# Two sets of seven products for a blocked second layer: which operands are summed first, and on which engine

## The chip, the cores and the metric

The kernel runs on one core of one Trainium2 chip. The metric is the device time of one execution in microseconds (us); the figure for a kernel is the median of its runs. The engines are named as in the profile: PE is TensorE (matmuls), PEld its weight loads, DVE is VectorE, ACT is ScalarE, POOL is GpSimd, SP is SyncE, which only issues transfers here.

## The reference, cut to what matters

```python
# q, k, v: 8 batches x 8 heads x 576 positions x 64
scores = scale * q @ k^T                      # per batch and head
ret    = (scores * Dmat) @ v                  # Dmat[i, j] = gamma_h ** (i - j) for i >= j, else 0
x      = ret, heads side by side              # 4608 tokens x 512
h      = x @ w_in                             # 512 -> 2048
g      = h * cos(h)
out    = g @ w_out                            # 2048 -> 512, float32
```

## The kernel before, in words

The 4608 tokens are worked off in ten stages, n = 0 to 9, of 512 tokens each but for n=1 and n=2, which have 256. A stage first runs the first layer (`mm1`, L365) in eight blocks. A block is 1024 columns of PSUM (two banks); in a late stage it holds two groups of 128 features by 512 tokens, eight matmuls in all. ScalarE takes the cosine (L373, as a sine with a shifted argument), VectorE multiplies (L374) and writes bf16 into the tile `gT`. Only then is the PSUM bank free. The blocks go round three bank pairs, `abmabmab`, so block i+3 waits for the multiplication of block i. The tile `gT` holds all 16 feature groups `et`. From n=4 on the order of the blocks alternates between the lower half of the features (`et` 0 to 7) and the upper half (8 to 15): blocks 0, 2, 4, 6 are the lower half, 1, 3, 5, 7 the upper.

From n=3 (`S7`) on the second layer is not computed as one product but by seven half-sized ones in the manner of Strassen. g is cut into quarters by token half (256 tokens each) and feature half, w_out into quarters by feature half and column half (256 columns each). Sums of quarters of w_out are made once (`w_sums`, L418), sums of quarters of g in each stage (`g_sum`, L445, tiles `gs..`). A product (`product`, L517) is 16 matmuls of 128x256 into one PSUM bank, `n` or `st`. In the kernel before the order is 3, 4, 5, 2, 1, 7, 6. Products 3 and 4 read `gT` itself; products 5, 2, 1, 7 and 6 each read a sum, so there are five sums a stage. Sum 5 is on VectorE, in two instructions of 1024 elements, one after block 3 and one late; nearly all of the other four go to GpSimd in instructions of 512 elements. The first GpSimd sum after a VectorE sum is made to wait for it (the `gate`). Where the results go, ScalarE copies three of them out of PSUM per stage (L557, L564, L569) and VectorE does six additions (L537, L559); the results leave in four stores (L544).

`sums_after(n, i)` places the sums behind block i. `late_sums(n)` places the second halves. `mm2_seven` issues the products; its `at` table hangs the attention work of later token groups between the products: `unit7` makes two state products (L266, VectorE sums `s` at L287), the attention output (L319, L333) and two groups of scores (L195), which VectorE masks (L207) into `ret`. With n=5 to 8 there are two such units; in n=3 and 4 a further group of scores comes first, and the last unit uses bank `b`. The list `pend` holds VectorE work that is issued at the next `flush`.

`store` issues a store on SP and calls `feed`, which for n>=3 prepares further token groups: three GpSimd instructions per group, scaling q (L140), scaling k (L140) and casting v (L156; on ScalarE for the last ten groups), one transposing DMA per group (L167) and loads of later groups (L117). SP issues in order, so a store that waits holds up the transposes and loads behind it. Each of `gT` and the `gs` tiles exists once. The schedule is the program's order on each engine.

Of the kernel before, what the change touches and what calls it, by code (L numbers as in the profile page):

```python
# [8 lines left out]
F32 = mybir.dt.float32  # L9
# [4 lines left out]
ALU = mybir.AluOpType  # L14
# [3 lines left out]
def kernel(  # L18
# [112 lines left out]
    def prep(g, early=False, kv_first=False):  # L131
# [20 lines left out]
        if early:  # L152
            tiles["fv", g] = fv
        else:
            copy_v = nc.scalar.copy if g > starts[S7] // P + 17 else nc.gpsimd.tensor_copy
            copy_v(vb, fv)  # L156
            if c == MIX and g > PER:
                copy_v(v_odd[HP:, g // PER % 2], fv[HP:])
# [245 lines left out]
    def w_sums(x, e0, e1):  # L404

        a, b, op_ = {
            3: ((0, 1), (1, 1), ALU.subtract),
            4: ((1, 0), (0, 0), ALU.subtract),
            1: ((0, 0), (1, 1), ALU.add),
            6: ((0, 0), (0, 1), ALU.add),  # L410
            7: ((1, 0), (1, 1), ALU.add),
        }[x]
        if x in (3, 4):
            w_sum[x] = w_quarter(*a)
        elif x not in w_sum:
            pool, tag = {1: (consts, "ws1"), 6: (first, "qs4"), 7: (first, "qT4")}[x]
            w_sum[x] = pool.tile([P, E2, N2], BF16, tag=tag, name=f"ws{x}")
        nc.vector.tensor_tensor(  # L418
            out=w_sum[x][:, e0:e1],
            in0=w_quarter(*a)[:, e0:e1],  # L420
            in1=w_quarter(*b)[:, e0:e1],
            op=op_,
        )

    def g_sum(n, x, e0, e1):

        gT = tiles["g", n]
        a, b, op_ = {
            5: ((0, 0), (0, 1), ALU.add),
            2: ((1, 0), (1, 1), ALU.add),  # L430
            1: ((0, 0), (1, 1), ALU.add),
            7: ((0, 1), (1, 1), ALU.subtract),
            6: ((1, 0), (0, 0), ALU.subtract),
        }[x]
        if ("gs", n, x) not in tiles:
            tiles["gs", n, x] = sump.tile([P, E2, 256], BF16, tag=f"gs{x}", name=f"gs{x}")
        on_dve = x == 5 or (n, x) == (S7, 2) or (n, x, e0) in (
            (S7, 1, 4), (last, 1, 0), (last, 2, 4)
        )
        step = e1 - e0 if on_dve else 2  # L440
        for e in range(e0, e1, step):
            i0, i1 = (
                gT[:, k * E2 + e : k * E2 + e + step, r * 256 : (r + 1) * 256] for r, k in (a, b)
            )
            i = (nc.vector if on_dve else nc.gpsimd).tensor_tensor(  # L445
                out=tiles["gs", n, x][:, e : e + step], in0=i0, in1=i1, op=op_
            )
            if on_dve:
                tiles["gate"] = i
            elif "gate" in tiles:  # L450
                tc.add_manual_dep(
                    i.ins,
                    tiles.pop("gate").ins.name,
                    mybir.DependencyInfo(mybir.DependencyClass.Sync, mybir.DependencyReason.DATA),
                    reason="port free",
                )

    def sums_after(n, i):

        if n == S7:  # L460
            if i < 4:
                w_sums(3 + i % 2, i // 2 * 4, i // 2 * 4 + 4)
            elif i < 6:
                g_sum(n, 5, i % 4 * 4, i % 4 * 4 + 4)
                if i == 5:
                    g_sum(n, 6, 0, 4)
            elif i == 7:
                g_sum(n, 2, 0, E2)
                g_sum(n, 1, 4, E2)
                g_sum(n, 1, 0, 4)  # L470
                for e in (0, 4):
                    g_sum(n, 7, e, e + 4)
                prep_next(kv_first=True)
                g_sum(n, 6, 4, E2)
        elif n == S7 + 1 and i in (3, 7):
            for x in (5, 2, 1):
                g_sum(n, x, i - 3, i + 1)
            for x in (7, 6) if i == 7 else ():
                for e in (0, 4):
                    g_sum(n, x, e, e + 4)  # L480
        elif i == 3:
            for x in (5, 2, 1, 7, 6) if n < last else (5, 1, 2, 7, 6):
                g_sum(n, x, 0, 4)
        elif i == 7 and n == last:
            late_sums(n)

    def late_sums(n):
        for x in (5, 2, 1, 7, 6):
            g_sum(n, x, 4, E2)

    def product(n, x):
# [3 lines left out]
        if x in (3, 4, 7) or (x == 1 and n < last):  # L495
            ps = psum.tile([P, 2, N2], F32, tag={3: "n", 4: "st", 1: "n", 7: "st"}[x], name="o")
            tiles["o", x] = [ps[:, j] for j in range(2)]
            tiles["all", x] = ps
        elif x == 1:
            ps = psum.tile([P, N2], F32, tag="n", name="o")  # L500
            pt = psum.tile([P, 2, 512], F32, tag="a", name="o")
            tiles["o", x] = [ps] + [pt[:, k, : N2 // 2] for k in range(2)]
        if x in (1, 6) and n == last:
            parts = [(0, 0, N2), (1, 0, N2 // 2), (1, N2 // 2, N2)]
        dst = tiles["o", {5: 3, 2: 4, 6: 1}.get(x, x)]
        lhs = {3: gT[:, :E2, :256], 4: gT[:, E2:, 256:]}.get(x)
        if lhs is None:
            lhs = tiles["gs", n, x]
        rhs = {5: w_quarter(1, 1), 2: w_quarter(0, 0)}.get(x)
# [5 lines left out]
        for e, i in order:  # L515
# [5 lines left out]
                start=(x in (3, 4, 1, 7) and e == 0 and (i == 0 or len(parts) > 2)),  # L521
# [5 lines left out]
    def mm2_seven(n, at):  # L527
# [8 lines left out]
        def add(out_, in0, in1, op_=ALU.add):  # L536
            pend.append(lambda: nc.vector.tensor_tensor(out=out_, in0=in0, in1=in1, op=op_))  # L537

        def new(tag):
            return op.tile([P, 2, N2], F32, tag=tag, name="ot")  # L540

        def store(t, r, c, s):
            r0 = starts[n] + r * 256
            nc.sync.dma_start(  # L544
                out[r0 : r0 + 256, c * N2 : (c + 1) * N2].rearrange("(j p) c -> p j c", p=P), t
            )
            feed(s)

        for x in (3, 4, 5, 2, 1, 7, 6):
            if x in at:  # L550
                at[x](flush, pend)
            else:
                flush()
            parts = product(n, x)
            if x == 3:
                u22 = new("a")
                nc.scalar.copy(u22, tiles["all", 3])  # L557
            elif x == 4:
                pend.insert(0, lambda: nc.vector.tensor_tensor(  # L559
                    out=u22, in0=tiles["all", 4], in1=u22, op=ALU.add  # L560
                ))
            elif x == 5:
                c12, u11 = new("c"), new("b")
                nc.scalar.copy(c12, tiles["all", 3])  # L564
                add(u11, u22, tiles["all", 3], ALU.subtract)
                store(c12, 0, 1, s0)
            elif x == 2:
                c21 = new("d")
                nc.scalar.copy(c21, tiles["all", 4])  # L569
                add(u22, u22, tiles["all", 4], ALU.subtract)  # L570
                store(c21, 1, 0, s0 + 1)
            elif x == 1 and n < last:
# [311 lines left out]
```

## Time and profile before

| what | value |
| --- | --- |
| time, median of three runs | 299.81 us (298.25 to 300.58) |
| span of the profiled execution, first to last instruction | 298.2 us |
| mean granted TensorE clock | 1.000 |
| busy: PE, DVE, ACT, POOL | 287.1, 207.9, 135.9, 209.4 us |
| sums of g on POOL (L445, 102 instructions) | 116.3 us, 1180 ns each |
| sums of g on DVE (L445, 18 instructions) | 20.4 us |
| multiplications into `gT` on DVE (L374, 72 instructions) | 87.8 us, 1223 ns each |
| final additions on DVE (L537 128x512 in two groups, and L559) | 13.1 + 9.6 + 4.8 us |

For the profiled execution only its span is given; it ran as long as the fastest of the three timed runs. A time of an engine is the union of its instructions; the matmuls' ends are modelled. In timeline lines the first number is the start in us from the begin of the span, the second the length in us, "x" the number of merged instructions, and the bracket tells how long the engine was idle before and what ended it. A line of the waits gives who waited for whom, the total in us, how often, and the longest.

### The profile page before, as it was taken

Reading aid. Unit: us, or ns where it says so; the run is one execution under the profiler, and the core shown is the slowest. Engines: PE = TensorE matmul, PEld = TensorE weight load, DVE = VectorE, ACT = ScalarE, POOL = GpSimd, SP = SyncE. Lnnn points to the kernel's source line nnn. Section 1 sums busy time; section 2 is a strip of 40 time slices with the busy share of each in tenths; the row PEclk is TensorE's granted clock in tenths of the full one; section 3 lists DMA queues with packets and bytes.
Section 4 is the critical chain, followed back from the end, with each engine's and each line's share of the span. In section 5 each row is a group of like instructions: output and inputs, shape, how many; then the busy total and the mean of one; then the engine's idle time right before and its main releaser. Section 6 shows DMA issues by size and latency. Waiting matters only on the chain.

```text
span 298.2 us, 7384 instructions
## 1 busy us (share of the span) xinstructions
PE 287.1 (96%) x3113; PEld 195.3 (65%) x3113; DVE 207.9 (70%) x245; ACT 135.9 (46%) x167; POOL 209.4 (70%) x214
## 2 busy tenths in 40 slices
PE   8899999999999999979999999999999999999995
PEld 3478646848578786448744875488448845874584
DVE  5677637564579994788848874887489757935872
ACT  2656433514255432642346554546464446425620
POOL 2750066436445599997999999599959946980693
PEclk9999999999999999999999999999999999999999
DMA  7999999999999999999999997998690260031013
GB/s 203 212 209 206 209 214 213 200 243 208 208 174 222 211 239 213 217 279 176 198 224 229 209 200 183 212 208 201 122 194 2 73 143 0 2 106 36 0 44 99
DMA packets 154304, 50.28 MB, mean 169 GB/s; under 512 B 140832, under 2 KB 153248, under 8 KB 154272
## 3 DMA queue, kind: packets, MB, share of 16 engines
q1 hardware_dynamic: 149504, 45.10, 77.2%
q0 software_dynamic: 4224, 4.19, 8.5%
q8 instruction: 24, 0.39, 0.6%
q10 hardware_dynamic: 544, 0.52, 0.5%
q14 instruction: 8, 0.07, 0.1%
HBM read 36.70 MB, written 9.44 MB: 155 GB/s over the span
## 4 chain that ended last, share of the span: by engine, by line
PE 43%; POOL 25%; SPq 13%; DMA 8%; DVE 5%; issue 3%; ACT 1%; POOLq 0%; DVEq 0%
PE h L365 22%; POOL gs L445 17%; PE o L517 11%; SPq L117 8%; POOL qks L140 6%; PE o L382 5%; SPq L167 4%; DVE gT L374 3%; DMA fk<-in_k_dram 2%; DMA w_in_sb<-in_moe_w_in_dram 2%; DMA qkT<-qks 2%; POOL vb L156 2%; DVE gs L445 2%; DMA fv<-in_v_dram 1%; ACT cosh L373 1%
## 5 line engine op out<-in xcount | busy, mean ns | idle before, releaser
L445 POOL TENSOR_TENSOR gs<-gT 128x512 bf16<-128x512 bf16 x102 | 116.3, 1180 | 29.4 <-DVE gs L445 29.4
L365 PE MATMUL h<-xT,w_in_sb 128*128 128x512 bf16 (+2 forms) x832 | 127.6, 313 | 2.6 <-DVE gT L374 1.8
L374 DVE TENSOR_TENSOR gT<-h,cosh 128x1024 bf16<-128x1024 f32 x72 | 87.8, 1223 | 43.7 <-ACT cosh L373 40.7
L373 ACT ACTIVATE cosh<-h,half_pi 128x1024 f32<-128x1024 f32 x72 | 80.2, 1114 | 72.2 <-PE h L365 69.8
L365 PEld LDWEIGHTS <-w_in_sb 128*128 128x128 bf16 x832 | 75.9, 98 | 51.6 <-issue 3.0
L140 POOL TENSOR_TENSOR qks<-fq,gq 128x512 bf16<-128x512 f32 x32 | 34.0, 1062 | 40.9 <-DMA fq<-in_q_dram 40.9
L517 PEld LDWEIGHTS <-gs 128*128 128x128 bf16 x576 | 53.6, 98 | 10.1 <-POOL gs L445 2.9
L140 POOL TENSOR_TENSOR qks<-fk,gk 128x512 bf16<-128x512 f32 x35 | 37.3, 1066 | 8.0 <-DMA fk<-in_k_dram 7.4
L207 DVE TENSOR_TENSOR ret<-sc,tri 128x1024 bf16<-128x1024 f32 x32 | 38.1, 1217 | 2.8 <-PE sc L195 2.7
L517 PE MATMUL o<-ws,gs 128*128 128x256 bf16 (+1 forms) x352 | 39.1, 268 | 0.7 <-POOL gs L445 0.5
L382 PE MATMUL o<-w_out_sb,gT 128*128 128x512 bf16 x128 | 30.1, 380 | 0.0
L517 PE MATMUL o<-w_out_sb,gT 128*128 128x256 bf16 x224 | 26.6, 273 | 0.1
L517 PE MATMUL o<-w_out_sb,gs 128*128 128x256 bf16 x224 | 26.1, 273 | 0.5 <-POOL gs L445 0.4
L537 DVE TENSOR_TENSOR ot<-o,ot 128x512 f32<-128x512 f32 (+2 forms) x25 | 14.9, 603 | 14.7 <-PE o L517 14.5
L517 PEld LDWEIGHTS <-gT 128*128 128x128 bf16 x224 | 21.4, 98 | 4.7 <-DVE gT L374 0.7
L350 ACT CAST xT<-ov 128x1024 bf16<-128x1024 f32 (+1 forms) x18 | 16.5, 917 | 16.1 <-PE ov L319 13.9
L445 DVE TENSOR_TENSOR gs<-gT 128x1024 bf16<-128x1024 bf16 (+1 forms) x18 | 20.4, 1148 | 0.3
L382 PEld LDWEIGHTS <-gT 128*128 128x128 bf16 x128 | 11.8, 98 | 12.5
L156 POOL CAST vb<-fv 128x512 bf16<-128x512 f32 x22 | 14.3, 651 | 4.4 <-DMA fv<-in_v_dram 4.2
L564 ACT COPY ot<-o 128x512 f32<-128x512 f32 x7 | 4.1, 586 | 20.5 <-PE o L517 20.5
L392 ACT COPY ot<-o 128x512 f32<-128x512 f32 x8 | 4.7, 588 | 17.4 <-PE o L382 17.4
L537 DVE TENSOR_TENSOR ot<-ot,o 128x512 f32<-128x512 f32 x14 | 9.6, 684 | 4.0 <-ACT ot L569 2.4
(70 smaller groups left out, 175.8 us busy)
## 6 DMA issues: line engine op xcount, KB each, us to landing
out_dram<-ot SPq DMA_DIRECT2D x35, 256.0 KB, 4.0
fk<-in_k_dram SPq DMA_DIRECT2D x32, 256.0 KB, 5.2
fv<-in_v_dram SPq DMA_DIRECT2D x32, 256.0 KB, 5.2
fq<-in_q_dram SPq DMA_DIRECT2D x30, 256.0 KB, 4.5
w_in_sb<-in_moe_w_in_dram POOLq DMA_DIRECT2D x4, 512.0 KB, 8.9
w_out_sb<-in_moe_w_out_dram POOLq DMA_DIRECT2D x4, 512.0 KB, 16.2
fq<-in_q_dram SPq DMA_DIRECT2D x8, 128.0 KB, 4.0
fk<-in_k_dram SPq DMA_DIRECT2D x8, 128.0 KB, 4.4
```

The costliest lines, as they stand in the source:

```text
L117: i = nc.sync.dma_start(f[p0:p1], src[b, :, s0 : s0 + p1 - p0, :].rearrange("h s d -> s h d"))
L140: eng.tensor_tensor(out=qks[:, m].rearrange("p (b a) d -> p a b d", a=2), in0=f.rearrange("p (a b) d -> p a b d", a=2), in1=by[:, c, :].re ...
L156: copy_v(vb, fv)
L207: nc.vector.tensor_tensor(out=ret.rearrange("p a b i -> p (a b) i"), in0=ps.rearrange("p a b i -> p (a b) i"), in1=mask.unsqueeze(1).to_br ...
L350: evac(tiles["x", n][:, :, t0 : t0 + len(gs) * P], ps.rearrange("p c x i -> p c (x i)"))
L365: nc.tensor.matmul(ps[:, j, :], lhsT=w_in_sb[:, dg, (et + j) * P : (et + j + 1) * P], rhs=xT[:, dg, c0 : c0 + w], start=(dg == 0), stop=(d ...
L373: nc.scalar.activation(cosh, ps, ACTF.Sin, bias=half_pi, scale=1.0)
L374: nc.vector.tensor_mul(gT[:, et : et + m, c0 : c0 + w], ps, cosh)
L382: nc.tensor.matmul(ps, lhsT=gT[:, et, tsi * P : (tsi + 1) * P], rhs=w_out_sb[:, et, :], start=(et == 0), stop=(et == ET - 1),)
L445: i = (nc.vector if on_dve else nc.gpsimd).tensor_tensor(out=tiles["gs", n, x][:, e : e + step], in0=i0, in1=i1, op=op_)
L517: nc.tensor.matmul(dst[i], lhsT=lhs[:, e, j * P : (j + 1) * P], rhs=rhs[:, e, c0:c1], start=(x in (3, 4, 1, 7) and e == 0 and (i == 0 or l ...
L537: pend.append(lambda: nc.vector.tensor_tensor(out=out_, in0=in0, in1=in1, op=op_))
```

## The change

Another set of seven products. Before each stage needed five sums of g; now it needs four, 5, 6, 7 and 3. Products 1, 2 and 4 read `gT` itself. Sums 5, 6 and 3 are on VectorE, and each of 6 and 3 reads the one made before it; only 7 is on GpSimd, and the gate between the engines is gone. The order of the products is 1, 2, 6, 4, 7, 5, 3. Products 6 and 7 go on adding into the bank that product 1 began; ScalarE copies that bank out after 1, after 6 and after 7, and bank `st` after 4: four copies, and five additions on VectorE. All four stores now follow an addition. Three sums of w_out are made beforehand and one in place in n=3. All casts of v in the late stages go to GpSimd. Line numbers shift: the sums of g become L437, the product L497, the additions L517, the multiplication L373, the first layer's matmul L364.

```diff
-            copy_v = nc.scalar.copy if g > starts[S7] // P + 17 else nc.gpsimd.tensor_copy
-            copy_v(vb, fv)
+            nc.gpsimd.tensor_copy(vb, fv)
...
     def w_sums(x, e0, e1):
...
+        a, b = {
+            5: lambda: (w_quarter(0, 1), w_quarter(0, 0)),
+            6: lambda: (w_quarter(1, 1), w_sum[5]),
+            4: lambda: (w_quarter(1, 0), w_sum[6]),
+            7: lambda: (w_quarter(1, 1), w_quarter(0, 1)),
+        }[x]()
...
     def g_sum(n, x, e0, e1):
+        def quarter(r, c):
+            return gT[:, c * E2 : (c + 1) * E2, r * 256 : (r + 1) * 256]
...
+        a, b, op_ = {
+            5: lambda: (quarter(1, 0), quarter(1, 1), ALU.add),
+            6: lambda: (tiles["gs", n, 5], quarter(0, 0), ALU.subtract),
+            7: lambda: (quarter(0, 0), quarter(1, 0), ALU.subtract),
+            3: lambda: (quarter(0, 1), tiles["gs", n, 6], ALU.subtract),
+        }[x]()
+        eng, step = (nc.gpsimd, 2) if x == 7 else (nc.vector, e1 - e0)
...
     def sums_after(n, i):
         if n == S7:
+            if i < 2:
+                w_sums(7, i * 4, i * 4 + 4)
+            elif i in (4, 5):
+                g_sum(n, 7, i % 4 * 4, i % 4 * 4 + 4)
+            elif i == 6:
+                for x in (5, 6, 3):
+                    g_sum(n, x, 0, 4)
+        elif i in (2, 4, 6):
+            g_sum(n, 7, i - 2 if i > 2 else 0, 4 if i == 2 else i)
+            if i == 6:
+                g_sum(n, 7, 6, E2)
         elif i == 3:
-            for x in (5, 2, 1, 7, 6) if n < last else (5, 1, 2, 7, 6):
+            for x in (5, 6, 3):
                 g_sum(n, x, 0, 4)
-        elif i == 7 and n == last:
-            late_sums(n)
+        elif i == 5:
+            for x in (5, 6, 3):
+                g_sum(n, x, 4, 6)
+
+    def late_sums(n, xs):
+        for x in xs:
+            g_sum(n, x, 4 if n == S7 else 6, E2)
...
     def product(n, x):
...
+        dst = tiles["o", 1 if x in (6, 7) else x]
+        lhs = {1: gT[:, :E2, :256], 2: gT[:, E2:, :256], 4: gT[:, E2:, 256:]}.get(x)
...
+        rhs = {1: w_quarter(0, 0), 2: w_quarter(1, 0), 3: w_quarter(1, 1)}.get(x)
...
-        for x in (3, 4, 5, 2, 1, 7, 6):
+        for x in (1, 2, 6, 4, 7, 5, 3):
...
+            if x == 6:
+                late_sums(n, (3,))
             parts = product(n, x)
+            if x == 1:
+                c11 = copied("a", 1)
+                if 2 not in at:
+                    late_sums(n, (5, 6))
+            elif x == 2:
+                pend[:0] = [add(c11, c11, tiles["all", 2]), store(c11, 0, 0, s0)]
+            elif x == 6:
+                u1 = copied("b", 1)
             elif x == 4:
+                c21 = copied("c", 4)
+            elif x == 7:
+                c22 = copied("d", 1)
+                pend += [add(c21, c21, tiles["all", 1]), store(c21, 1, 0, s0 + 1)]
             elif x == 5:
+                pend += [
+                    add(c22, c22, tiles["all", 5]),
+                    add(u1, u1, tiles["all", 5]),
+                    store(c22, 1, 1, s0 + 2),
+                ]
+            elif n < last:
+                pend += [add(u1, u1, tiles["all", 3]), store(u1, 0, 1, s0 + 3)]
                 flush()
...
                 at = {
-                    4: lambda then, off: unit7(g, "st", True, lambda: late_sums(n), off),
-                    1: lambda then, off: unit7(g + 2, "n", True, then),
+                    2: lambda then, off: unit7(g, "st", True, lambda: sums_then(then), off),
+                    5: lambda then, off: unit7(g + 2, "st", True, then),
                 }
                 if n in (3, 4):
                     at = {
-                        5: lambda then, off: (then(), scores2(g)),
-                        1: lambda then, off: unit7(g, "n", True, then),
-                        6: lambda then, off: unit7(g + 2, "b", n > 3, then),
+                        6: lambda then, off: (then(), scores2(g)),
+                        5: lambda then, off: unit7(g, "st", True, then),
+                        3: lambda then, off: unit7(g + 2, "b", n > 3, then),
                     }
```

## The prediction

> **What bounds the kernel now.** I read the busy shares first, then the 40 slices, then one late stage in the window view and the timeline, then the list of waits.
>
> ```profile
> PE 287.1 (96%) x3113; PEld 195.3 (65%) x3113; DVE 207.9 (70%) x245; ACT 135.9 (46%) x167; POOL 209.4 (70%) x214
> PE   8899999999999999979999999999999999999995
> 209.19:238.62 29.43, 29.43 (x338) 19.82 (x336) 21.95 (x24) 14.95 (x19) 26.40 (x25) 1.00 0.45 99
> ```
>
> The second row shows TensorE busy in tenths; the third is stage n=7 alone (length, then busy time of PE, PEld, DVE, ACT and POOL, clock, DMA share, GB/s). TensorE is busy for all 29.43 us. Nothing another engine saves there can shorten the stage, and whatever makes TensorE wait is added to the end.
>
> ```profile
> PEld L517 <- POOL gs L445: 2.9, 7, 0.7
> PE h L365 <- DVE gT L374: 1.8, 1, 1.8
> ```
>
> These waits (total, times, longest) are what a change of the sums can give back. I bound it by phase lengths from the timeline. The products with their attention units take 15.54 us in n=6. Against that, a score group counted as 0.57, the excess is 1.69 in n=3, 1.20 in n=4, 0.65 in n=5, 0.08 in n=7 and 0.40 in n=8; n=9 (13.02 us, no units) exceeds 112 matmuls at 0.1115 by 0.53. First-layer blocks take 13.81, but 15.75 in n=4: 1.94 more. In all 6.4 us.
>
> **Room in the first-layer phase.** A stage runs eight blocks of eight matmuls (0.2158 each, 1.727 a block). ScalarE makes the cosine, VectorE multiplies, and only the product frees the PSUM bank. With three banks in turn, block 7 needs product 4 finished.
>
> ```profile
> 209.19 13.98 PE L365 MATMUL h<-xT,w_in_sb 128*128 128x512 bf16 x64
> 217.44 1.23 DVE L374 TENSOR_TENSOR gT<-h,cosh 128x1024 bf16<-128x1024 f32 x1 [0.50 <-ACT cosh L373]
> 218.70 0.69 DVE L445 TENSOR_TENSOR gs<-gT 128x1024 bf16<-128x1024 bf16 x1
> 219.31 1.22 DVE L374 TENSOR_TENSOR gT<-h,cosh 128x1024 bf16<-128x1024 f32 x1
> 220.90 1.23 DVE L374 TENSOR_TENSOR gT<-h,cosh 128x1024 bf16<-128x1024 f32 x1 [0.37 <-ACT cosh L373]
> 222.62 1.23 DVE L374 TENSOR_TENSOR gT<-h,cosh 128x1024 bf16<-128x1024 f32 x1 [0.50 <-ACT cosh L373]
> ```
>
> Columns: start, length, instruction. Block 7 is due at 209.19 + 56 x 0.2158 = 221.27. Product 4, behind one sum, ends at 220.53. The room is 0.74 us. Two rows check it:
>
> ```profile
> 277.32 1.29 DVE L445 TENSOR_TENSOR gs<-gT 128x1024 bf16<-128x1024 bf16 x2
> 126.30 3.33 DVE L445 TENSOR_TENSOR gs<-gT 128x1024 bf16<-128x1024 bf16 x1
> 130.81 0.38 PE L365 MATMUL h<-xT,w_in_sb 128*128 128x512 bf16 x1 [1.78 <-DVE gT L374]
> ```
>
> In n=9 two sums (0.60 more) fit, and TensorE does not pause. In n=4 one sum took 3.33, which is 2.64 more; less 0.74 that makes 1.90, and TensorE waited 1.78.
>
> **What the change removes.** POOL's sums fall from 102 to 34 (four in n=3, five in each of six stages; the one issued at i=4 repeats e=2 to 4), so 68 x 1.157 = 79 us leave POOL; ten casts (0.651) and a v_odd copy (0.85) come to it, 7.4 us. POOL does not bound a late stage, so this is worth only part of the 6.4 us above. I take 1.94 for n=4's first-layer phase, 0.70 for n=4's products (0.5 is scores waiting for bank b, which the change keeps), 0.65 for n=5, 0.40 for n=8, 0.50 for n=9 and 0.50 for n=3: its new wait, product 6 behind the second halves of two sums and scores b behind a late product 7, costs 0.6 to 1.5 of its 1.69. Gain 4.7, bounds 3.0 and 6.4.
>
> Off the path: ScalarE gets seven more copies (4.1 us) and loses ten casts (6.2); it has about 14 us idle a stage. VectorE loses a final add per stage (0.685 each) and two weight sums (0.74 each). TensorE issues eight fewer, smaller matmuls in the last stage: under 0.2 us. If VectorE or ScalarE had no such idle time the final adds would count, because product 4 waits in bank st for the add of product 2; I return to it.
>
> SyncE: the stores now wait for VectorE adds where two of four waited for ScalarE copies. The second goes from about 22 to 27 us into the stage, and behind it queue a transpose and three loads of that feed. Those groups are used a stage later, so I cost it at nothing. Without that lead its price is up to the 5 us once, in n=3 or n=4, where DMA is near its limit.
>
> **What it adds on the path: VectorE's sums.** In each of n=4 to 9, three chained sums of 1024 elements follow block 3 where one stood, and three of 512 follow block 5. Alone one of 1024 takes 0.69; each waits for the one before, about 0.03 more, so 0.72. No sum of 512 is in the trace. A sum takes 0.69 for 1024; the one of 2048 took 1.48, of which it stood 0.40 behind a POOL instruction, so 1.08; so one of 512 lies between half of 0.69 (0.35) and 0.69 less half of that step (0.49). I take 0.41, and 0.44 with the gap.
>
> First set, alone: 218.70 + 3 x 0.72, product 4 at 220.75 to 221.98, block 7 at 222.03 instead of 221.27: 0.76 late.
>
> Then the collision. Sums on VectorE stretch when POOL is working:
>
> ```profile
> 226.28 1.67 DVE L445 TENSOR_TENSOR gs<-gT 128x1024 bf16<-128x1024 bf16 x1
> 219.57 18.33 POOL L445 TENSOR_TENSOR gs<-gT 128x512 bf16<-128x512 bf16 x16 [3.03 <-DVE gs L445]
> ```
>
> VectorE's sum at 226.28 took 1.67 amid POOL's run, of which one instruction of 1.16 explains all but 0.5. The ordering between sums of the two engines (the gate) is gone. POOL's first gs7 instruction follows product 0; the second follows product 2 (216.95) and 0.18 of waking; the third, the repeat, follows at once: 217.13, 218.25, end about 219.4. The first VectorE sum, due at 218.70, ends near 219.92 instead of 219.39: 0.53 more. First wait: 1.29 us (bounds 0.76, and 2.45 if a second POOL instruction gets in).
>
> Second set: product 4 ends at 222.51, product 5 at 223.66, three sums to 225.0, product 6 at 226.16. TensorE finishes block 7 at 224.29 and starts the new product 1, which reads g of blocks 0, 2, 4, 6; its thirteenth matmul, due at 225.63, needs product 6. It waits 0.57. Alone the two waits are 0.76 + 0.65 = 1.41; with one collision 1.29 + 0.57 = 1.86.
>
> Behind it VectorE still has product 7, two state sums, two half sums, a mask (1.21) and the add that frees bank st. I count that add as about 0.9 us early for product 4 if POOL stays away and up to 0.65 late if POOL's preparations take turns with the half sums (n=5 to 7). I take 0.2 us in those three.
>
> **Sum.** 6 x 1.86 + 3 x 0.2 = 11.8 lost, 4.7 gained: +7.1 us on a span of 298.2, so 305.3. The profiled execution is as short as the fastest run (298.25); the median is 299.81, 1.6 above. On the median: 306.9. Low: 6 x 1.41 - 6.4 = +2.1, 301.9. High: 6 x 1.86 + 3 x 0.65 + 4 x 1.16 (one more POOL instruction in each of n=4 to 7) - 3.0 = +14.8, 314.6.
>
> The Trainium skill, "SBUF — State Buffer", section "SBUF: two separate sides", says that VectorE and GpSimd share a port pair as an exclusive lock for a whole instruction, the later one being fully blocked; it speaks against moving sums to VectorE while GpSimd works. The 1.67 row agrees, and so does 3.33. Read as chance, by the page, each of six sums would wait on average half a POOL instruction (0.58) for POOL's share of 0.57 (16.8 of 29.4 us): an estimated 2.0 a stage instead of 0.45, and about 316 in all; I go by where POOL stands at that moment.
>
> **Rivals.**
> 1. *Waits vanish, nothing takes their place.* The sums after block 3 fit the room. For it: two fit in n=9. Against: three need 2.16, and room and one sum make 1.43; it decides if a chained sum costs under 0.48. Then 299.8 - 4.7 = 295.1: faster.
> 2. *POOL wins again and again,* as at 126.30, where one sum outwaited three POOL instructions. Where preparations run on into the next first-layer phase (n=4 to 7), two more of 1.16 per stage: 306.9 + 9.3 = 316.2. Against it: with 72 us less on POOL, preparations should end within their stage.
> 3. *The change costs what it gives.* Both low losses and high gains, +2.1 or a little less: about 301.5. For it: 6.4 us of pauses are really there. Against: those of n=3 and part of n=4 have causes that stay.
>
> **How the numbers follow.** Forecast 0.70, rival 1 0.07, rival 2 0.10, rival 3 0.13. The time is the forecast's, 306.9. The range 301.0 to 313.5 takes in rival 3 and most of the unknown collisions; rivals 1 and 2 stay outside. One per cent, 3 us, is about what a measurement tells from no change. Faster 0.06 (most of rival 1), same 0.13 (most of rival 3 and the rest of 1), slower 0.81.
>
> **What would show it.** Right: in n=4 to 9, TensorE pauses of 0.8 to 1.5 us before block 7, released by gT, and of about 0.6 in product 1; VectorE above 85% there; POOL near 138 us; POOL out of the list of TensorE's waits. First sums of a set near 1.2 show the collision, 0.69 its absence. Wrong: late stages still 29.4 us long with no pause at gT, or pauses released by ot adds, DMA or POOL instead.

## The result and the profile after

The changed kernel takes 315.54 us (median of four runs, 314.97 to 316.26). The kernel before, run beside it, takes 300.19 us (298.25 to 303.07). The ratio is 1.054, with a 95% interval of 1.050 to 1.058. The forecast was 306.9 us and slower: the side was right and the size was not, since the time lies above the range as well. Ratios leave out runs more than about 1.5% above the fastest of their kernel; this matters in experiment 4, where five of ten runs took 301.23 to 302.63 us at a mean clock of 0.988 to 0.994, and none of those was profiled, so what they waited for is open.

The page of the kernel after, engines' busy time, the granted clock by slices, and the shares of the chain that ended last:

```profile
PE 291.0 (93%) x3105; PEld 196.8 (63%) x3105; DVE 223.8 (71%) x276; ACT 134.1 (43%) x163; POOL 141.0 (45%) x157
PEclk9999999999899979999999999999999999999999
PE 39%; DVE 19%; ACT 2%; issue 1%; DVEq 0%
```

GpSimd's work fell from 209.4 to 141.0 us, as forecast (138). VectorE's rose by 15.9 us, and the last row shows what that means: a fifth of the chain now runs through VectorE (5% before). The clock row has two slices, the 11th and the 15th, in which TensorE was not given its full clock; no slice before was like that.

The waits (who waits for whom, total, times, longest):

```profile
PE h L364 <- DVE gT L373: 7.4, 7, 1.2
PEld L497 <- DVE gT L373: 4.4, 6, 0.7
PE o L497 <- DVE gT L373: 2.7, 6, 0.5
PE sc L194 <- DVE gT L373: 1.7, 1, 1.7
PE sc L194 <- DMA qkT<-qks: 1.6, 1, 1.6
```

GpSimd's sums, which of all other engines' work held TensorE longest before (2.9 us in total), are gone from the list. The first three rows are the two pauses of a late stage, six times each; the first row has one more, of 0.48 us, in n=3. The last two are single pauses outside of the late stages, and they turn out to be expensive. Stage n=7, in the timeline: VectorE's part, then GpSimd's, then TensorE's.

```profile
228.70 1.23 DVE L373 TENSOR_TENSOR gT<-h,cosh 128x1024 bf16<-128x1024 f32 x1 [0.50 <-ACT cosh L372]
229.96 1.26 DVE L437 TENSOR_TENSOR gs<-gT 128x1024 bf16<-128x1024 bf16 x1
231.25 0.69 DVE L437 TENSOR_TENSOR gs<-gs,gT 128x1024 bf16<-128x1024 bf16 x1
231.98 0.69 DVE L437 TENSOR_TENSOR gs<-gT,gs 128x1024 bf16<-128x1024 bf16 x1
232.59 2.35 DVE L373 TENSOR_TENSOR gT<-h,cosh 128x1024 bf16<-128x1024 f32 x2
234.97 0.42 DVE L437 TENSOR_TENSOR gs<-gT 128x512 bf16<-128x512 bf16 x1
...
228.28 2.39 POOL L437 TENSOR_TENSOR gs<-gT 128x512 bf16<-128x512 bf16 x2 [2.17 <-DVE gT L373]
...
233.86 1.89 PE L364 MATMUL h<-xT,w_in_sb 128*128 128x512 bf16 x8 [1.16 <-DVE gT L373]
237.51 0.61 PE L497 MATMUL o<-w_out_sb,gT 128*128 128x256 bf16 x4 [0.45 <-DVE gT L373]
```

The first sum starts at 229.96 and takes 1.26 instead of 0.69, because GpSimd's second instruction of the pair (the repeat) runs until 230.67. Three sums stand between multiplications 3 and 4, and block 7 (the eight matmuls at 233.86) starts late. Then three short sums hold multiplication 6, which the last four matmuls of product 1 need. Both pauses are where and about as long as the prediction put them.

A table of stretches shows what they come to. The length of a phase is the safer measure than the bracketed idle time, because the ends of matmuls are modelled: the pause reads 1.16, and the phase is 1.32 longer. "After" is the profiled execution of the result, "again" that of the same kernel in experiment 8.

| stretch, us | before | after | again |
| --- | --- | --- | --- |
| start of n=3 | 84.18 | 87.39 | 84.39 |
| n=3, first layer | 15.37 | 16.00 | 15.37 |
| n=3, products | 17.24 | 21.25 | 22.30 |
| n=4, first layer | 15.75 | 15.13 | 15.22 |
| n=5 to 9, first layer, each | 13.81 | 15.13 | 15.13 |
| n=4 to 9, products in all | 93.04 | 95.28 | 95.28 |
| span | 298.2 | 314.6 | 312.1 |

From "before" to "again" the products of n=3 cost 5.1 us, and everything from n=4 on 8.6 (with 0.27 at the tail). The prediction had -0.5 for the first and +7.6 for the second. So the late stages were read well, and n=3 was not. In the execution "after", 3.2 us more went before n=3.

What happened in n=3, from the kernel after (GpSimd's sums and its first preparation, VectorE's sums, and where TensorE goes on after its two pauses):

```profile
100.72 4.50 POOL L437 TENSOR_TENSOR gs<-gT 128x512 bf16<-128x512 bf16 x4
...
104.26 1.50 DVE L437 TENSOR_TENSOR gs<-gT 128x1024 bf16<-128x1024 bf16 x1
105.80 0.69 DVE L437 TENSOR_TENSOR gs<-gs,gT 128x1024 bf16<-128x1024 bf16 x1
105.83 1.56 POOL L140 TENSOR_TENSOR qks<-fq,gq 128x512 bf16<-128x512 f32 x1 [0.61 <-DMA fq<-in_q_dram]
106.53 1.42 DVE L437 TENSOR_TENSOR gs<-gT,gs 128x1024 bf16<-128x1024 bf16 x1
109.13 0.42 PE L194 MATMUL sc<-qkT 64*64 64x128 bf16 x16 [1.72 <-DVE gT L373]
109.97 1.42 DVE L437 TENSOR_TENSOR gs<-gs,gT 128x1024 bf16<-128x1024 bf16 x1
111.45 1.89 PE L497 MATMUL o<-ws,gs 128*128 128x256 bf16 x8 [0.92 <-DVE gs L437]
```

GpSimd goes from its four sums through a wait of 0.61 us into preparations (L140), so VectorE's sums meet its instructions: of the six of n=3, three take 1.42 to 1.50 instead of 0.69 and two 0.83 and 0.98. In "again" five of the six take 1.30 to 1.53. GpSimd pays too (1.56 instead of 1.04). The three sums come before multiplication 7, which scores b wait for (1.72), and the late sums hold the second half of product 6 (0.92). Then the clock falls. The same kernel in windows (length, busy times of PE, PEld, DVE, ACT, POOL, granted clock, DMA share, GB/s):

```profile
84.00:87.30 3.30, 3.30 (x23) 1.39 (x24) 1.92 (x2) 0.00 (x0) 1.35 (x2) 0.50 1.18 186
111.50:114.70 3.20, 3.20 (x16) 2.28 (x17) 3.20 (x4) 0.59 (x1) 2.40 (x4) 0.51 1.25 241
```

TensorE is busy and works at half its clock. The first stretch, 83.89 to 87.30 in full, follows a wait of 1.62 us for a transposed tile (qkT) at the end of n=2; the second, 111.19 to 114.61, follows the pauses of 1.72 and 0.92. Each costs about half its length, 1.7 us.

### The profile page after: what moved, and what is told of

The parts are those of the page before. It is cut to its first block, busy times and chain, and to the rows that moved or that the text cites. A ratio compares the mean times of both kernels' runs of the same rounds, so it can differ in the third digit from the quotient of the medians.

```text
span 314.6 us, 7334 instructions
## 1 busy us (share of the span) xinstructions
PE 291.0 (93%) x3105; PEld 196.8 (63%) x3105; DVE 223.8 (71%) x276; ACT 134.1 (43%) x163; POOL 141.0 (45%) x157
## 4 chain that ended last, share of the span: by engine, by line
PE 39%; DVE 19%; ACT 2%; issue 1%; DVEq 0%
PE o L497 21%; PE h L364 13%; DVE gT L373 9%; DVE gs L437 8%; ACT cosh L372 2%; PE ov L332 1%; PE sc L194 1%; PE st L265 1%; DVE ot L517 1%; PE ov L318 1%; DVE ret L206 1%; DVE s L286 1%; ACT ot L521 0%; DVEq L864 0%; DVEq L286 0%
## 5 line engine op out<-in xcount | busy, mean ns | idle before, releaser
L364 PE MATMUL h<-xT,w_in_sb 128*128 128x512 bf16 (+2 forms) x832 | 128.6, 313 | 8.1 <-DVE gT L373 7.4
L373 DVE TENSOR_TENSOR gT<-h,cosh 128x1024 bf16<-128x1024 f32 x72 | 86.9, 1221 | 39.0 <-ACT cosh L372 36.5
L364 PEld LDWEIGHTS <-w_in_sb 128*128 128x128 bf16 x832 | 75.9, 98 | 58.5 <-issue 10.7
L437 POOL TENSOR_TENSOR gs<-gT 128x512 bf16<-128x512 bf16 x34 | 39.2, 1157 | 93.1 <-DVE gT L373 92.6
L140 POOL TENSOR_TENSOR qks<-fq,gq 128x512 bf16<-128x512 f32 x32 | 34.6, 1081 | 50.3 <-DMA fq<-in_q_dram 48.0
L497 PEld LDWEIGHTS <-gs 128*128 128x128 bf16 x456 | 43.5, 99 | 7.5 <-DVE gs L437 1.2
L140 POOL TENSOR_TENSOR qks<-fk,gk 128x512 bf16<-128x512 f32 x35 | 38.9, 1110 | 10.0 <-DMA fk<-in_k_dram 9.3
L497 PEld LDWEIGHTS <-gT 128*128 128x128 bf16 x336 | 32.5, 99 | 10.0 <-DVE gT L373 4.4
L521 ACT COPY ot<-o 128x512 f32<-128x512 f32 x28 | 16.4, 587 | 49.0 <-PE o L497 47.7
L517 DVE TENSOR_TENSOR ot<-ot,o 128x512 f32<-128x512 f32 x34 | 22.6, 681 | 12.3 <-ACT ot L521 8.4
L497 PE MATMUL o<-w_out_sb,gT 128*128 128x256 bf16 x224 | 27.3, 273 | 2.7 <-DVE gT L373 2.7
L497 PE MATMUL o<-ws,gs 128*128 128x256 bf16 x224 | 27.8, 278 | 1.2 <-DVE gs L437 0.9
L497 PE MATMUL o<-w_out_sb,gs 128*128 128x256 bf16 (+1 forms) x232 | 26.8, 269 | 0.0
L381 PEld LDWEIGHTS <-gT 128*128 128x128 bf16 x128 | 12.1, 100 | 13.4 <-issue 1.5
L437 DVE TENSOR_TENSOR gs<-gT 128x512 bf16<-128x512 bf16 (+1 forms) x20 | 16.1, 805 | 0.5
L437 DVE TENSOR_TENSOR gs<-gs,gT 128x512 bf16<-128x512 bf16 (+1 forms) x20 | 14.3, 713 | 0.7
L194 PE MATMUL sc<-qkT 64*64 64x128 bf16 (+1 forms) x480 | 11.0, 220 | 3.6 <-DVE gT L373 1.7
```

Of the source, the lines that this page charges most:

```text
L140: eng.tensor_tensor(out=qks[:, m].rearrange("p (b a) d -> p a b d", a=2), in0=f.rearrange("p (a b) d -> p a b d", a=2), in1=by[:, c, :].re ...
L364: nc.tensor.matmul(ps[:, j, :], lhsT=w_in_sb[:, dg, (et + j) * P : (et + j + 1) * P], rhs=xT[:, dg, c0 : c0 + w], start=(dg == 0), stop=(d ...
L373: nc.vector.tensor_mul(gT[:, et : et + m, c0 : c0 + w], ps, cosh)
L381: nc.tensor.matmul(ps, lhsT=gT[:, et, tsi * P : (tsi + 1) * P], rhs=w_out_sb[:, et, :], start=(et == 0), stop=(et == ET - 1),)
L437: eng.tensor_tensor(out=tiles["gs", n, x][:, e : e + step], in0=a[:, e : e + step], in1=b[:, e : e + step], op=op_,)
L497: nc.tensor.matmul(dst[i], lhsT=lhs[:, e, j * P : (j + 1) * P], rhs=rhs[:, e, c0:c1], start=(fresh and e == 0 and (i == 0 or len(parts) > 2)),
```

## The experiments

The theory that the expectations call A: the loss is VectorE's sums themselves, through the pauses they cause before block 7, in product 1 and in n=3, all lengthened by GpSimd instructions that run at the same time; the late start of n=3 is chance. Against it stand other causes: the later start of n=3 belongs to the change, or stores, additions and copies cost the time.

**1. The kernel before once more.** No edit. Is the start of n=3 as fixed as it looks?

> The kernel before, unchanged, profiled a second time. The changed kernel starts its stage n=3 3.05 us later than the kernel before did (87.39 against 84.34), behind a wait of 1.62 us for a transposed tile (qkT) at the end of n=2, where the programs hardly differ. Theory A, that wait is a draw of the transfers' timing and not the change's: this profile may show any start of n=3 between 84.3 and 87.5, and the time lies anywhere between 298 and 303. Theory B, the change causes it: n=3 starts at 84.3 to 84.5 again, with a wait under 0.2 us, and the span is 298.0 to 298.6.

It took 301.3 us, with a span of 299.6. Its n=3 starts at 85.55 instead of 84.18 (the expectation has 84.34, the timeline 84.18), after this wait at the end of n=2:

```profile
83.68 0.42 PE L195 MATMUL sc<-qkT 64*64 64x128 bf16 x16 [1.00 <-DMA qkT<-qks]
```

So the kernel before draws that wait too: none in one execution, 1.00 in the other. Experiment 8 looks at it from the other side.

**2. GpSimd's sums without the repeat.** The sum of i=4, which only repeats one of i=2, is left out, so that GpSimd is given two instructions after block 2 and two after block 6.

```diff
-        elif i in (2, 4, 6):
-            g_sum(n, 7, i - 2 if i > 2 else 0, 4 if i == 2 else i)
-            if i == 6:
-                g_sum(n, 7, 6, E2)
+        elif i in (2, 6):
+            g_sum(n, 7, 0 if i == 2 else 4, 4 if i == 2 else E2)
```

> The changed kernel without GpSimd's repeated instruction: sum 7 is made behind blocks 2 and 6 alone. Theory A, VectorE's first chained sum stands behind that instruction: it falls from 1.25 to 0.69 us in n=4 to 9, TensorE's pause before block 7 from 1.16 to 0.60, the one in product 1 stays near 0.45 to 0.5, and six stages give 3.0 to 3.4 us: about 312.3. Rival, the 1.25 has another cause (the first read of fresh g): it stays, and the time stays at 315 to 316.

Measured: 311.95 us (311.69 to 312.34), ratio 1.039 (1.036 to 1.042). In n=5 to 9 the first-layer phase is 14.56 to 14.58 instead of 15.13:

```profile
230.92 1.89 PE L364 MATMUL h<-xT,w_in_sb 128*128 128x512 bf16 x8 [0.59 <-DVE gT L373]
```

The three sums there take 0.69 each. So 0.76 of the 1.32 are the sums alone, and 0.56 is the collision with the repeat; the prediction had 0.76 and 0.53. The pause in product 1 is untouched. In n=4 the phase is 16.19: GpSimd is late there, its two sums now meet VectorE's (1.48 and 1.53), and block 7 waits 2.21. Its n=3 takes 22.24 and is as bad as ever.

**3. n=3's sums moved behind.** The first halves of sums 5 and 6 come after block 7 instead of block 6, and sum 3 as a whole behind the late sums 5 and 6, just ahead of product 6 in the program.

```diff
-            elif i == 6:
-                for x in (5, 6, 3):
+            elif i == 7:
+                for x in (5, 6):
                     g_sum(n, x, 0, 4)
 ...
             if x == 6:
+                if n == S7:
+                    g_sum(n, 3, 0, 4)
                 late_sums(n, (3,))
```

> The changed kernel with VectorE's sums of stage n=3 moved from behind block 6 to behind block 7, and sum 3 made whole just before product 6. Theory A, these sums hold up multiplication 7, thereby scores b and product 6, and the two pauses (1.72 and 0.92) put TensorE at half clock for some 3 us: the pause of 1.72 is gone, a wait of 0.4 to 1.1 in product 6 stays, the granted clock stays at 1.00 from 100 to 125 us, and the products of n=3 take 17 to 18.5 instead of 21.25 us: 312 to 313. Rival, GpSimd's preparations or late loads bound n=3: the pauses only move, and the time falls by less than 1 us.

Measured: 314.03 us (312.89 to 316.12), ratio 1.047 (1.042 to 1.052), against the 312 to 313 expected; the interval overlaps that of the changed kernel, so no gain is shown. Scores b no longer wait, but product 6 does, twice:

```profile
105.14 1.05 PE L497 MATMUL o<-ws,gs 128*128 128x256 bf16 x8 [0.93 <-DVE gs L437]
108.14 1.05 PE L497 MATMUL o<-ws,gs 128*128 128x256 bf16 x8 [1.96 <-DVE gs L437]
```

The sums of 5 and 6 took 1.05, 1.53, 1.63 and 1.42 amid GpSimd's sums and preparations. The products of n=3 came to 19.84 (17 to 18.5 expected), 2.5 less than in "again", at a clock of 1.00 in spite of 2.9 us of pauses; but the first layer of n=4 went from 15.22 to 15.69 and its products from 17.74 to 18.65. So the wait moved with the sums. Order alone doesn't mend n=3 while GpSimd works beside them.

**4. The products without VectorE's sums.** All instructions of GpSimd, the copies, additions and stores of the change stay. Products 5, 6 and 3 read quarters of g.

```diff
+        if x != 7:
+            return
...
+        if x in (3, 5, 6):
+            lhs = gT[:, :E2, 256:] if x == 3 else gT[:, E2:, 256:] if x == 5 else gT[:, :E2, :256]
```

> The changed kernel without VectorE's sums 5, 6 and 3: products 5, 6 and 3 read quarters of g instead, so the output is not the reference's; all else, with GpSimd's sum 7, four copies and the new stores, stays. Theory A, these sums are the whole loss of n=3 to 9: no pause before block 7 and none in product 1, first-layer phases of 13.8 instead of 15.13, products of n=6 and 7 at 15.5 instead of 16.1 to 16.25: 6 x 1.6 and some 4.5 in n=3 less, 300 to 302 with the late start of n=3, 297 to 299 without. Rival, part of the loss lies with the later stores, the additional copies or bank st: 304 or more, with pauses ended by ot or DMA.

Measured: 297.49 us in the median of the five runs in the ratio (296.67 to 298.41), 299.82 over all ten; ratio 0.991 (0.988 to 0.993). Its stage n=7 in the profiled run, of 297.49 us:

```profile
207.50:236.93 29.43, 29.43 (x338) 19.89 (x336) 19.19 (x22) 14.49 (x18) 10.88 (x11) 1.00 0.47 104
```

TensorE is busy all the time, as before the change. All first-layer phases from n=4 on are 13.81 or 13.82, and n=3's products take 16.71 (17.24 before). One late stage has a new pause: in n=5 the products take 17.10 (16.19 before), because TensorE stands before the second half of a scores group whose tile qkT landed at 165.70:

```profile
165.75 0.26 PEld L194 LDWEIGHTS <-qkT 64*64 64x64 bf16 x16 [1.44 <-DMA qkT<-qks]
```

Whether the later stores cause this, or only that TensorE is there earlier, is not separated. So in the profiled run the loss is VectorE's sums and what they bring with them: the added copies, the final additions and the wait for bank `st` cost nothing that shows, and the four stores behind additions at most this one pause. Without a cost of VectorE's sums the change would have won about 0.9%.

**5. Room for two sums.** Experiment 2's kernel, with only sums 5 and 6 after blocks 3 and 5; sum 3 is made in one piece of six feature groups before product 6.

```diff
-            for x in (5, 6, 3):
+            for x in (5, 6):
                 g_sum(n, x, 0, 4)
 ...
-            for x in (5, 6, 3):
+            for x in (5, 6):
                 g_sum(n, x, 4, 6)
 ...
             if x == 6:
+                if n > S7:
+                    g_sum(n, 3, 0, 6)
                 late_sums(n, (3,))
```

> The changed kernel without GpSimd's repeat, and in n=4 to 9 with only two chained sums (5 and 6) behind block 3 and behind block 5; sum 3 is made whole before product 6. A test of the room of 0.74 us before block 7. Theory A: two sums of 0.69 with 0.03 between them, alone on the port, take 0.72 more than the one of the kernel before, just what the room holds: the pause before block 7 (1.16 in the changed kernel, 0.59 without the repeat) is 0 to 0.1; behind it two sums of 0.43 make product 6 about 0.2 late for product 1. 0.8 to 0.9 less per stage than without the repeat (311.95): 306.5 to 308 if n=3 and n=4 stay as they are. Rival, TensorE waits for something else there as well: a pause of 0.3 or more before block 7 stays.

Measured: 303.48 us (303.11 to 304.08), ratio 1.012 (1.009 to 1.015), better than the 306.5 to 308 expected, because n=4's first-layer phase fell as well (14.56, from 16.19 in experiment 2) and the products of n=4 to 9 take 3.1 us less in all. The first-layer phases of n=5 to 9 are 13.84. From n=4 on, the first layer's matmuls wait for gT only once, for 0.6 us in n=4.

Two chained sums fit and three don't: with two the phases are 0.03 longer than before the change, with three 0.76 (experiment 2), so the room of 0.74 us in the prediction is confirmed from both sides. (With two sums multiplication 4 ends at 225.57 in n=7, and block 7 is due at 213.50 + 56 x 0.2158 = 225.58.) The pause in product 1 is nearly gone as well, and sum 3 later in the stage costs little: n=7's products take 15.79, against 15.62 in experiment 4. What stays is n=3, 22.71 us.

**6. Only sum 5 early.** From experiment 2's kernel: in all stages sum 5 alone stays in the first-layer phase, sums 6 and 3 follow in the products, and the mask of the first scores of a unit may wait.

```diff
-            for x in (5, 6, 3):
-                g_sum(n, x, 0, 4)
+            g_sum(n, 5, 0, 4)
 ...
+            if x == 5:
+                g_sum(n, 5, 4 if n == S7 else 6, E2)
+            else:
+                g_sum(n, x, 0, 4)
+                g_sum(n, x, 4, E2)
 ...
-            scores(g, "a", parts=2)
+            scores(g, "a", parts=2, put_off=put_off)
```

> The changed kernel with sums 6 and 3 made wholly after product 1 and before product 6, only sum 5 in the first-layer phase (as in the kernel before), in n=3 sum 5's first half behind block 6; no repeat on GpSimd; both masks of a unit put off behind the add that frees bank st. Theory A: in n=5 to 9 no pause before block 7 and none over 0.1 in product 1, which takes back 1.5 us of each stage; while GpSimd prepares in the same time, the late sums stretch to 1.0 to 1.6 each and bank st is free late, 0 to 0.6 per stage; n=3 keeps 2 to 3 of its 4.8 us: 303 to 306. Rival, only the amount of VectorE's work counts and not its place: the pauses reappear at bank st or in product 6 with 1 us or more per stage, and the time stays over 309.

Measured: 302.63 us (300.89 to 303.37), ratio 1.007 (1.004 to 1.010), a little under the 303 to 306 expected. The first-layer phases are 13.81 everywhere, n=4 included. In n=5 and n=7 the products take 16.43, 0.8 us more than in experiment 7, because the late sums now meet GpSimd's preparations:

```profile
227.14 1.08 DVE L437 TENSOR_TENSOR gs<-gT 128x512 bf16<-128x512 bf16 x1
228.15 2.54 DVE L437 TENSOR_TENSOR gs<-gs,gT 128x1024 bf16<-128x1024 bf16 x2
```

**7. The same, with GpSimd held back.** The first preparation of a stage (L140) waits for the last instruction of sum 6.

```diff
+            if x == 6:
+                tiles["gate"] = i
 ...
+            if "gate" in tiles:
+                tc.add_manual_dep(i.ins, tiles.pop("gate").ins.name, ...)
```

> As e6_sums_late, and GpSimd's first preparation of a stage waits for the last instruction of sum 6 on VectorE, so that the two do not meet. Theory A, meeting on a port is what stretches the late sums: those of 1024 elements fall to 0.69 us in n=4 to 7 and those of n=3 behind product 1 to 0.7 to 1.1; n=3's products fall to 17 to 18 us: 1 to 3 us less than e6_sums_late, 300 to 303. Rival, GpSimd's preparations are themselves what the scores wait for, and holding them costs as much as the sums gain: equal to e6_sums_late within 1 us, with pauses ended by qkT or qks.

Measured: 300.65 us (299.28 to 301.96), ratio 1.002 (1.000 to 1.005): no difference from the kernel before. The same sums of n=7, and the preparation that waits for them:

```profile
227.66 0.42 DVE L444 TENSOR_TENSOR gs<-gT 128x512 bf16<-128x512 bf16 x1
228.00 1.29 DVE L444 TENSOR_TENSOR gs<-gs,gT 128x1024 bf16<-128x1024 bf16 x2
...
229.36 1.04 POOL L140 TENSOR_TENSOR qks<-fq,gq 128x512 bf16<-128x512 f32 x1 [2.90 <-DVE gs L444]
```

The two sums of sum 6 take 1.29 instead of 2.54, and the products of n=5 and n=7 take 15.62. The number and the order of VectorE's sums are the same in both; it is the meeting with GpSimd's instructions that stretches them. In n=3 the gate doesn't help, because there it is GpSimd's own four sums, 5.38 us in one run, that VectorE's sums meet (1.63, 1.51, 1.63): the products take 21.0 us (17 to 18 expected, 19.62 in experiment 6), with a pause of 2.55 and a stretch at half clock.

**8. The changed kernel once more.** No edit; run beside experiment 9.

> The changed kernel, unchanged, profiled a second time. Its first profile started n=3 at 87.39, after a wait of 1.62 us for qkT and some 3.3 us at half clock; six kernels that share its program up to there started n=3 at 84.3 to 84.7 with waits of 0.3 to 0.7. Theory A, the late start is a draw: this profile starts n=3 near 84.5, and the time is 312 to 314 with the rest unchanged (n=3 about 20 to 22 us of products, late stages 15.13). Theory B, it belongs to this kernel: 87 again and 315 to 316.

Measured: 315.14 us (313.76 to 315.77), ratio 1.051 (1.048 to 1.054); the profiled run took 313.76, within the 312 to 314 expected, the median lies above. Of the late start of n=3 nothing is left: 84.39, with a wait of 0.23 for qkT instead of 1.62. So it is a draw and not fixed in this kernel, as theory A had it. The products of n=3, however, are 1 us longer than in the result's profile (pauses of 2.45 and 1.49): on this stage executions differ. The profiled run was the fastest of the four. Its mean clock is 0.995, which is one stretch of 3.4 us at half clock (1.7 of 312 us); in the other three the mean is 0.987, two stretches or more, and they take 1.1 to 2.0 us longer. Where these lie is not known, since they have no profile. In the kernel before, run with experiment 1, the listed clocks are 0.998 to 1.000.

**9. Less meeting in n=3.** Experiment 7's kernel; the blocks of n=3 are reordered so that GpSimd's sums can begin one block earlier, and one cast of v moves behind them.

```diff
-                halves.sort()
+                halves = [(0, 0), (0, 4), (0, 8), (1, 0), (1, 4), (0, 12), (1, 8), (1, 12)]
 ...
-            elif i in (4, 5):
-                g_sum(n, 7, i % 4 * 4, i % 4 * 4 + 4)
+            elif i in (3, 4):
+                g_sum(n, 7, i % 3 * 4, i % 3 * 4 + 4)
+                if i == 4:
+                    nc.gpsimd.tensor_copy(tiles["a", 15][1], tiles.pop(("fv", 15)))
```

> As e7_sums_late_gate, and in n=3 the order of the blocks brings GpSimd's sum 7 forward (behind blocks 3 and 4), ahead of the cast of v of group 15, so that it is done before VectorE's sums behind product 1. Theory A, in n=3 too it is the meeting of the two engines that costs: the four late sums of n=3 fall to 0.69 each, product 6 waits under 0.6 us instead of 2.55, the clock stays at 1.00, and n=3's products take 16.8 to 17.6 instead of 21.0: 296 to 297.5, faster than the kernel before. Rival, n=3 is bound by the transfers (qkT, fq) at that point: products stay over 19 us with pauses ended by DMA, and the time stays at 299 or more.

Measured: 298.81 us (298.06 to 300.04, twelve runs), the kernel before 300.18 beside it, ratio 0.996 (0.994 to 0.998). This version beats both kernels, by 1.4 us over the one before.

```profile
98.17 4.95 POOL L444 TENSOR_TENSOR gs<-gT 128x512 bf16<-128x512 bf16 x4
...
104.14 1.28 DVE L444 TENSOR_TENSOR gs<-gs,gT 128x1024 bf16<-128x1024 bf16 x2
104.88 1.92 PE L507 MATMUL o<-ws,gs 128*128 128x256 bf16 x16 [0.78 <-DVE gs L444]
```

GpSimd's sums begin at 98.17 (100.75 in experiment 7) and end at 103.12, sum 6 takes 1.28 for its two instructions, the pause ahead of product 6 is 0.78 instead of 2.55, and the clock stays at 1.00. Sum 5 still meets GpSimd (1.37 and 0.95). n=3's products take 17.86, 3.1 less than in experiment 7: 1.8 of pause and 1.7 of half clock that are gone, less small losses. The order of n=3's blocks changed along with the meeting, so its own share is not separated. n=3's products are still 1.15 above experiment 4: the pause of 0.78 and one of 0.94 before the last unit, which waits for a mask; only one product lies between the last two units in the new order, where two did. In n=5 the products take 16.12 against 15.62 in experiment 7, with a wait of 0.30 for qkT. The 296 to 297.5 expected was missed by a little over 1 us in the median. The slower of the runs have spans up to 298.3 at the same clock; they have no profile, so what they waited for stays open.

## Why the prediction was right or wrong

*The room, 0.74 us, and the sums alone, 0.76.* Right. Experiment 2 has the phases 0.76 longer (14.57 against 13.81), experiment 5 shows that two sums fit.

*The collision, 0.53.* Right: 0.56, from 15.13 less 14.57. The whole first pause, predicted at 1.29, is 1.32 by the phase. It didn't spread: no second GpSimd instruction got in, in any late stage's first layer.

*Sums of 512 elements, 0.41, and the pause in product 1, 0.57.* The duration was right (0.42 to 0.43), the pause a little long (0.45).

*Chance against position.* By position I had 1.86 us a stage, and 1.32 + 0.45 = 1.77 came. Where GpSimd stood was known, and going by it was right. In the rows here a collision is paid by the one that comes second: 0.69 becomes 1.26 to 1.63 on VectorE, 1.16 about 1.6 and 1.04 about 1.5 on GpSimd. The exclusive lock that the Trainium skill describes ("SBUF — State Buffer", section "SBUF: two separate sides") agrees with these rows. The reading by chance, put at 2.0 us a stage, took GpSimd's share as 16.8 of 29.4 us; in n=7 it came to 11.28 of 31.38, with which the same reading gives an estimated 1.25, still twice the 0.56 measured.

*Gains from n=4 on, 4.2 of the 4.7.* Partly right. The first-layer pause of n=4 went (15.75 less 1.94, plus 1.32, is the 15.13 measured). In the products I counted 0.70 for n=4 and 0.65 for n=5; both stages are longer by 0.44 and 0.41, which is the new pause in product 1, so these gains are nil. n=8 gave 0.23 and n=9 0.43 of the 0.40 and 0.50. The missed 1.6 us were partly made up by the second pause, 0.12 shorter in each stage, and by bank `st`: I counted 0.2 for it in n=5 to 7, and beyond the 0.45 n=6 and n=7 are longer by 0.07 and 0.18, which no experiment took apart. In all +8.6 where I had +7.6.

*SyncE, stores and additions at nothing.* Right for the changed kernel as far as its waits show; without VectorE's sums one wait for a tile of 1.44 us comes up in n=5 (experiment 4).

*n=3: "its new wait, product 6 behind the second halves of two sums and scores b behind a late product 7, costs 0.6 to 1.5 of its 1.69".* This is the step that failed. The wait was named, with both its places, and mis-sized: 3.9 us of pauses in "again" (2.45 and 1.49) and 1.7 us of half clock, so that the stage's products grew by 5.1 where I had them shrink by 0.5. The prediction gives no working for this price, and its only collision terms are those of n=4 to 9. The profile before shows what was left out; this is its window of the products of n=3:

```profile
99.55:116.79 17.24, 16.58 (x275) 13.43 (x273) 14.31 (x19) 6.12 (x10) 15.36 (x15) 1.00 1.20 244
```

GpSimd is busy for 15.36 of 17.24 us and VectorE for 14.31. Work that GpSimd's instructions stretch could not be put here at its undisturbed duration. I made the collision count for the late stages alone, where GpSimd is busy for 5.8 to 21.9 of some 31 us (kernel after), and left it out for the one where it hardly rests. That the meeting makes the wait long is shown directly in n=5 and n=7 (experiment 7); in n=3 it is shown by experiments 3, 4 and 9 together, and in the main.

*The clock.* There was no term for it, and that is the second part of the miss. The mean clock of the changed kernel's four runs of the result is 0.988 to 0.989, which is 1.1 to 1.2% of 314 us, so some 3.6 us; the profile's two stretches are two times 1.7, of which the one in n=3 is counted above. The late start of n=3 (3.2 us in that profile, of which about half is such a stretch) is in neither the second profile nor those of experiments 2 to 7. But seven of the eight runs of this kernel have a mean clock (0.987 to 0.989) that stands for two stretches or more, so a second one is common here, and where it lies in the runs without a profile is open.

*Rival 2, 316.2, is close to the time, but not by its reason.* It had GpSimd winning again and again in the first-layer phases of n=4 to 7. These phases are 15.13, as forecast. GpSimd did win repeatedly in the products of n=3, where neither forecast nor rival had a collision. Rival 1 is refuted by the pauses; rival 3 needed losses of 1.41 a stage, and they were 1.77 and more.

*The offset of 1.6 us* between span and median was right in size and wrong in reason: each run lists its span, and the time is always about 1.7 us above it (316.26 and 314.6). So the profile before, with its span of 298.2, came from a run of about 299.8, the median, and not from the fastest.

*Slips in the sums.* The pauses before add up to 6.49, not 6.4. The second pause "alone", 0.65, does not follow from the working, which gives 0.57 with the collision and without, as both its ends move by the same 0.53; experiment 2 measured 0.45. Together they would lower the low bound by 0.6 us; the forecast stays.

*What was to show it.* The two pauses, their releasers, GpSimd's 141 us and the first sums at 1.26 came as described. VectorE "above 85%" did not: it is busy for 11.55 of the 15.13 us of n=7's first-layer phase, 76%. It has idle time before block 3 and none after it, so an average of the phase was the wrong thing to name.

## What to carry to other kernels

Before work is moved to an engine, read in each stage, not only in the typical one, what the engine that disturbs it does at that moment; a sum on VectorE beside a working GpSimd took about twice its time alone here (1.26 to 1.63 against 0.69 us), and a chain of sums can pay that at each step. Ask of every chain put between two steps of a pipeline how many links fit into the room (here two of three); the link beyond it could stand later at little cost (experiment 5). A wait can be repaired by moving it only if what makes it long doesn't move along: here the sums had to go later and GpSimd had to be held off.

## What the hardware showed that was not expected

TensorE's clock falls after pauses much shorter than I would have guarded against. Pauses of 1.62 us (end of n=2), 1.72 and 0.92 (n=3), 2.45 and 1.49 (experiment 8) and 2.55 (experiment 7), and in n=3 also 2.17 and 1.59 (experiment 2) and 2.73 and 1.49 (experiment 5), were followed by 3.41 us at a granted clock of 0.50. Six pauses of 1.16 were not, nor was one of 1.78 in the kernel before, nor 0.93 and 1.96 in experiment 3, nor 2.21 in n=4 of experiment 2. So the length of the pause alone does not decide.

The Trainium skill, "TensorE: Matmul & The Clock Gate", section "Why this matters for your kernels", advises against idle gaps of TensorE over about 3 us. No single gap here was that long, and the clock fell all the same. Its section "What's actually happening" has the clock go by the activity in a free-running window of 3.41 us. The traces agree with the grid: in every profile here the clock changes only at whole multiples of 3.413 us from its first rise, in the kernel after at 5.38, 83.89, 87.30, 111.19 and 114.61, and a lowered stretch inside the run lasts one such step. What makes it fall is less clear. A natural reading is that a pause counts by how much of one step it fills, and the pause of 2.21, which lies across two steps, fits it. So do five falls: TensorE was idle for 2.0 us of the step before in four of them and for 2.55 in the fifth. But these two steps speak against each other (length, then busy times as above):

```profile
80.48:83.89 3.41, 1.84 (x58) 1.21 (x56) 1.84 (x5) 1.01 (x1) 2.60 (x3) 1.00 1.06 149
106.20:109.61 3.41, 1.47 (x14) 1.32 (x15) 3.38 (x4) 0.38 (x1) 3.41 (x4) 1.00 1.26 229
```

In the first, from the kernel after, TensorE was idle for 1.57 us and the clock fell at its end. In the second, from experiment 3, it was idle for 1.94 us and the clock stayed. So the idle share of a step does not decide alone either; what else counts stays open, and no run here shifted a pause against the grid.
